# New transfer and matmul estimates in a list planner, and a reserve that now holds for every engine

## The chip, the core and the metric

The kernel runs on one core of a Trainium2 chip. The time is the device time of one execution in microseconds; the median of three runs is given. PE is the matrix engine, DVE, ACT and POOL are the vector, scalar and GpSimd engines, and SP is the engine whose queue issues all transfers here.

## The reference

Two layers are run, each an attention block and a Fourier block, both with a residual and a layer norm in front:

```python
x = A_x                                   # 2048 x 512, 32 heads of 16, 4 segments of 512 rows
for _ in range(2):
    x = x + A(layernorm(x), wq, wk, wv, wo, beta)
    x = x + B(layernorm(x), dft_seq_re, dft_seq_im, dft_hid_re, dft_hid_im)

def A(x, ...):                            # for each segment s, with the memory M, z of those before it
    p = softmax(q_s @ k_s.T * scale + mask);  a_dot = p @ v_s
    a_mem = (phi(q_s) @ M) / (phi(q_s) @ z + 1e-6)
    o_s = g * a_mem + (1 - g) * a_dot
    M, z = M + phi(k_s).T @ v_s, z + sum(phi(k_s))
    # phi(t) = t + 1 where t > 0, else exp(t);   result: concat(o) @ wo

def B(x, ...):                            # real part of a two-dimensional DFT, as matmuls
    a, b = x @ hid_re.T, x @ hid_im.T
    return seq_re @ a - seq_im @ b
```

## The kernel before

**The work.** Eight heads make a group, so a layer has 4 segments x 4 groups and the program 32 groups, numbered i = 0 to 31 (16 to a layer). A group passes through generator functions, each of which yields what it needs next and then issues instructions:

- `s_ln`/`t_ln` normalise four 128-row tiles of a segment and transpose them by a transfer (tile `g`).
- `s_p` multiplies by the q and k weights, `t_split` cuts the product into two fp16 halves, writes them to DRAM (`d<-w`) and reads them back in another layout (`qst<-d`, `kst<-d`). `t_phi` and `t_phk` form phi; `t_phk` starts from a transposed copy of k (tile `kt`, shown as `w<-w`), which POOL adds, ACT and DVE scale, and POOL adds again.
- `s_x` makes scores for the row maxima: PE writes a PSUM tile (kind `ss`, at most 4 held), and `t_max` on DVE takes the maximum with the mask (`junk<-b,cmask`, then `mx`). A transpose of `mx`, two small instructions on `mhl` and four small transfers put the maxima into `qst`. `s_st` then makes the scores again, ACT takes the exponential, POOL cuts the upper triangle (`t_sel`), and `s_av` multiplies by v.
- `s_m` and `t_merge` divide: the denominators go out and come back as [128, 32] (`den<-w` twice, `dc<-den`), DVE takes the reciprocal, `rec<-dc` writes it, `w<-rec` reads it back spread over partitions (tile `z`, kind `mz`), and POOL or DVE multiplies. `s_o` applies `wo`.
- `s_ab`, `s_c`, `s_r`, `s_f` are the Fourier block: `s_c` prepares the sequence matrix, `s_f` multiplies piece by piece into `y` through `t_y`. Of these matmuls there are plenty, and they need little else, so they stand between the others where they can ("the filler", below).

**What sets the order.** No order is written out by hand. A planner runs while the program is built. `Plan.op` keeps for each engine the time at which it is free and for each tile the times of its last write and read, by an estimated cost for each instruction. `Plan.ready` gives the estimated time at which a generator's next step has its inputs and buffers. The loop at the end of `body` always issues the step whose estimated start is earliest. What it issues goes to the end of its engine's queue, and each engine runs its own queue in that order. So a wrong estimate changes no result and no amount of work; it only places an instruction in a queue ahead of one that could have run.

A transfer's estimate in `Plan.op` is issue time `c`, 650 ns, the bytes at 360 bytes per ns on one shared resource `D`, and a `tail`. `est=(c, tail)` sets both at a call. `RESERVE` adds 1000 ns to the readiness of tiles that a transfer wrote and 500 ns to those that POOL wrote, but only where the waiting step is one of PE:

```python
RESERVE = dict(G=500.0, Y=1000.0, V=0.0, A=0.0)
...
            r = max(r, self.wr.get(n, 0.0) + (RESERVE.get(self.by.get(n), 0.0) if eng == "T" else 0.0))
```

All instructions are recorded through one helper (`call` in `Eng`), so the profile puts nearly all of them on line 237; they are told apart by their tiles.

Of the kernel before, what the change touches and what calls it, by code (L numbers as in the profile page):

```python
# [8 lines left out]
F32R = mybir.dt.float32r  # L9
# [30 lines left out]
class Plan:  # L40


    LAT = dict(T=197.0, V=150.0, A=165.0, G=100.0, Y=0.0)

    def __init__(self):
        self.free = dict.fromkeys("VGATYD", 0.0)
        self.acc = {}
        self.cols = {}
        self.wr = {}
        self.rd = {}  # L50
        self.area, self.count, self.slot = {}, {}, {}
        self.fresh = set()
        self.fine = {}
        self.by = {}
        self.dma = None
        self.mode, self.units, self.begun, self.entered = "m", {}, 0.0, 0.0

    def turn(self, mode):
# [65 lines left out]
    def ready(self, reads, tags, eng):  # L124
        r = self.slots_free(tags)
        if r is None:
            return None
        for t in reads:
            n = self.key(t)
            if n in self.fresh:  # L130
                return None
            r = max(r, self.wr.get(n, 0.0) + (RESERVE.get(self.by.get(n), 0.0) if eng == "T" else 0.0))
        return r

    def op(self, eng, name, args, kw):
        aps = [a for a in list(args) + list(kw.values()) if isinstance(a, bass.AP)]
        out, ins = [aps[0]], aps[1:]
        if name == "tensor_tensor_reduce":
            out.append(ins.pop())
        n = max(a.free_size() for a in aps)  # L140
        lat = self.LAT[eng]
        src = any(a.space == bass.MemoryType.PSUM for a in ins)
        if eng == "T":
            n, w = out[0].free_size(), aps[1]
            slow = 4 if w.dtype == F32 else 1
            c = n / 2.4 * slow + (18 if w.dtype == F32R else 3)
            cols = n * slow * w.partition_size() / 128
            mode, unit = "m", 0
            if name == "matmul" and out[0].partition_size() == 32:
                mode, unit = "v", out[0].start_partition() // 32  # L150
            elif w.partition_size() <= 64:
                mode, unit = "h", w.start_partition() // 64
        elif eng == "A":
            c = n / 1.2 + (52 if src else 93) + (93 if any(a.free_size() == 1 for a in ins) else 0)
        elif eng == "V":
            c = 68 + n / 0.96
            if name == "reciprocal":
                c = 68 + n * 6.25
            elif name == "scalar_tensor_tensor" and out[0].dtype == F32:
                c += 60  # L160
            elif name == "tensor_copy" and out[0].dtype == F16:
                c = 68 + n / 1.92
            elif name == "tensor_scalar" and out[0].dtype == F32:
                c = 68 + n / (0.87 if src else 1.32)
        elif eng == "G":
            c = 127 + n * 0.915 if name == "affine_select" else 96 + n * 2.2
            if name == "tensor_tensor" and kw.get("op") == OP.pow:
                c = 300 + n * 165
            elif name == "partition_all_reduce":
                c = 370  # L170
        else:
            stored = out[0].space == bass.MemoryType.DRAM
            c, tail = self.dma or (440, 350 if stored else 950)
            if kw.get("transpose"):
                c, tail = 1350, 450
        t = self.free[eng]
        for a in ins:
            t = max(t, self.wr.get(self.key(a), 0.0))
        for o in out:
            m = self.key(o)  # L180
            t = max(t, self.rd.get(m, 0.0))
            if eng == "V" and "reduce" not in name or self.by.get(m, eng) != eng:
                t = max(t, self.wr.get(m, 0.0))
        psum = [self.key(a) for a in aps if a.space == bass.MemoryType.PSUM]
        for m in psum:
            for o, u in self.acc.get(m, {}).items():
                if o != eng:
                    t = max(t, u)
        if eng == "T":
            if mode == self.mode:  # L190
                t = max(t, self.begun + 7, self.units.get(unit, 0.0))
            else:
                t = max(t, max(self.units.values(), default=0.0) + SWITCH)
                self.mode, self.units, self.entered = mode, {}, t
            k = int(t / TICK)
            if self.cols.get(k - 1, 0) < 3060:
                c = min(2 * c, max(c, (k + 1) * TICK - t + c / 2))
            self.cols[int((t + c) / TICK)] = self.cols.get(int((t + c) / TICK), 0) + cols
        e = t + c
        self.free[eng] = e  # L200
        if eng == "T":
            self.begun = t
            self.units[unit] = e
            if len(self.units) < dict(m=1, h=2, v=4)[mode]:
                self.free[eng] = t + 7
            else:
                self.free[eng] = min(self.units.values())
        if eng == "Y":
            self.free["D"] = max(self.free["D"], e + 650) + out[0].nbytes() / 360
            e = self.free["D"] + tail  # L210
        e += lat
        for m in psum:
            self.acc.setdefault(m, {})[eng] = e
        for a in ins:
            m = self.key(a)
            self.rd[m] = max(e, self.rd.get(m, 0.0))
        for o in out:
            m = self.key(o)
            self.wr[m] = e
            self.by[m] = eng  # L220
            self.fresh.discard(m)
        for a in ins + out:
            if a.tensor.name in self.slot:
                ar, b = self.slot[a.tensor.name]
                ar["last"][b] = max(ar["last"][b], e)
# [18 lines left out]
def body(ctx: ExitStack, tc: tile.TileContext, x, wq, wk, wv, wo, beta, wd, cs, out):  # L244
# [303 lines left out]
    def t_merge(e, o, gi, g, n, key):  # L548
        yield gate("GM")
        yield need("A", e, o, gm, tag=("md", "md"))  # L550
        ds = []
        for src in (e, o):
            d = sb("md")
            A.activation(d, src, AF.Copy)
            ds.append(d)
        A.activation(n, e, AF.Copy, scale=gm[:, gi, 0, g:g + 1])
        yield need("V", n)
        V.scalar_tensor_tensor(n, o, gm[:, gi, 1, g:g + 1], n, op0=OP.mult, op1=OP.add)
        pl.close(e, o)
        yield need("Y", *ds)  # L560
        den = tc.dram_tile([NP, 2, 512], F32)
        rec = tc.dram_tile([NP, 2, 512], F32)
        for a, d in enumerate(ds):
            Y.dma_start(den[:, a, :], d[16 - 16 * a:128:32, :], est=(530, 500))
        pl.close(*ds)
        yield need("Y", den)
        c = rg("dc", 3, F32, (128, 32))
        Y.dma_start(c, den.rearrange("p a (x c) -> (p a x) c", c=32), est=(350, 750))
        yield need("V", c)
        if not gi:  # L570
            V.tensor_scalar(c, c, 1e-6, None, op0=OP.add)
        V.reciprocal(c, c)
        yield need("Y", c)
        Y.dma_start(rec.rearrange("p a (x c) -> (p a x) c", c=32), c, est=(380, 450))
        yield need("Y", rec, tag="mz")
        z = sb("mz")
        Y.dma_start(z, rec.rearrange("p a n -> (p a) n").unsqueeze(1).to_broadcast([2 * NP, 16, 512]),
                    est=(650, 2100))
        yield need("VG", n, z)
        tt(n, n, z, OP.mult)  # L580
        pl.close(z)
        done.add(key)

    def t_split(p, key, f, kphi):
# [16 lines left out]
        yield need("Y", hl)  # L601
        d = tc.dram_tile([2, 2, 64, 512], F16)
        for a in range(2):
            Y.dma_start(d[a].rearrange("j p n -> p j n"), hl[64 * a:64 * a + 64], est=(670, 800))
        pl.close(hl)
        i = key[1]
        if i >= NR:
# [6 lines left out]
        for a in range(2):  # L614
            f = d[a].rearrange("j (d p) n -> (j d) (p n)", p=NP)
            o = dst[64 * a:64 * a + 64].rearrange("r p n -> r (p n)")
            if order:
                Y.dma_start(o[0:32], f, est=(420, 1300))
                Y.dma_start(o[32:48], f[0:16], est=(420, 1300))
            else:  # L620
                Y.dma_start(o[0:16], f[0:16], est=(420, 1300))
                Y.dma_start(o[16:48], f, est=(420, 1300))
        done.add(key)

    def t_phi(p, hl, r, f, key):
# [151 lines left out]
    def s_x():  # L777
        for i in range(NGRP):
# [30 lines left out]
            for a in range(2):  # L809
                for j in range(2):  # L810
                    r = 64 * a + 62 + j
                    Y.dma_start(qs[r:r + 1].rearrange("o p (t n) -> o (p t) n", t=TT),
                                mhl[16 * a:16 * a + 16, j, :], est=(610, 500))
            done.add(("X", i))

    def t_sel(sp, pt, w, n, f, keys):
# [347 lines left out]
```

## Time and profile before

| | us |
|---|---|
| runs | 1836.32, 1828.71, 1827.49 |
| median | 1828.71 |
| span of the profiled execution, first to last instruction | 1824.8 |
| PE busy in the span | 1697.8 (93%) |
| DVE, ACT, POOL busy | 1085.9, 897.1, 724.6 |
| transfers' share of the 16 engines | 47% |

The time of the profiled execution itself isn't listed beside the runs; its span is 3.9 us under their median. PE is the busiest engine by far, and from about 1572 us on it works alone with the filler. PE's own row "PEclk" gives the granted clock, which is under 1 in places early and around 1000 to 1125 us.

### The profile page before, as it was taken

How to read it: one execution, taken by the hardware profiler on the slowest of the kernel's cores; microseconds unless marked ns; L12 is line 12 of the kernel's file. 1: busy time of each engine (PE TensorE's matmuls, PEld its weight loads, DVE VectorE, ACT ScalarE, POOL GpSimd, SP SyncE). 2: the span in 40 equal slices, each digit the busy share in tenths (PEclk: the TensorE clock that was granted, in tenths of full speed). 3: DMA queues.
4: the chain of work that ended last, by engine and by line, in shares of the span. 5: the costliest groups of instructions: out<-in, count | busy, mean ns of one | idle time of the engine just before them, and what ended most of it. 6: DMA issues, size and time to landing. Idle time of an engine off the chain costs nothing. (4 is left out here: it accounts for less than half of the span.)

```text
span 1824.8 us, 32643 instructions
## 1 busy us (share of the span) xinstructions
PE 1697.8 (93%) x11045; PEld 742.2 (41%) x11045; DVE 1085.9 (60%) x3404; ACT 897.1 (49%) x1563; POOL 724.6 (40%) x1158
## 2 busy tenths in 40 slices
PE   3878799989989999999999879999999999999999
PEld 2433334443433434344444333434444434444444
DVE  7786955577765877565556655564656567533211
ACT  2557656757465666644436655555445444431000
POOL 3234545546363464553434543442534334231000
PEclk8988899999999999999999898999999999999999
DMA  7345535655454653345784541553544444222233
GB/s 190 105 135 132 170 74 165 156 152 150 127 147 136 191 149 102 119 151 167 232 226 156 136 124 49 144 131 100 132 110 114 141 120 102 83 84 81 93 122 115
DMA packets 240985, 242.44 MB, mean 133 GB/s; under 512 B 129777, under 2 KB 152305, under 8 KB 240817
## 3 DMA queue, kind: packets, MB, share of 16 engines
q1 hardware_dynamic: 240816, 240.35, 46.9%
q8 instruction: 87, 1.43, 0.3%
q14 instruction: 82, 0.66, 0.1%
HBM read 152.96 MB, written 63.70 MB: 119 GB/s over the span
## 5 line engine op out<-in xcount | busy, mean ns | idle before, releaser
L237 PEld LDWEIGHTS <-w 128*128 128x128 f16 x4992 | 463.8, 98 | 613.3 <-issue 113.0
L237 PE MATMUL b<-w,w 128*128 128x512 f16 x3072 | 708.9, 380 | 2.0 <-ACT w L237 1.7
L237 POOL TENSOR_TENSOR w<-w,w 128x512 f16<-128x512 f32 (+1 forms) x316 | 380.6, 1208 | 412.6 <-ACT w L237 266.9
L237 ACT ACTIVATE w<-b,fac 128x512 f32<-128x512 f32 (+1 forms) x728 | 420.9, 658 | 176.6 <-PE b L237 156.0
L237 DVE CUSTOM_DVE_ANT_0 junk<-b,cmask 128x128 bf16<-128x128 f32 (+3 forms) x1024 | 437.6, 485 | 77.7 <-PE b L237 76.3
L237 POOL TENSOR_SCALAR_AFFINE_SELECT w<-w 128x128 f32<-128x128 f32 (+2 forms) x704 | 242.4, 357 | 309.5 <-ACT w L237 302.6
L237 DVE SCALAR_TENSOR_TENSOR y<-b,fyu,y 128x512 f32<-128x512 f32 x200 | 149.2, 746 | 217.7 <-PE b L237 217.2
L237 ACT ACTIVATE w<-b 128x512 f32<-128x512 f32 (+1 forms) x240 | 138.2, 600 | 251.9 <-PE b L237 240.4
L237 ACT ACTIVATE w<-w,csc 128x512 f16<-128x512 f32 (+1 forms) x256 | 181.1, 721 | 60.7 <-DVE csc L237 51.5
L237 PE MATMUL b<-g,w 128*128 128x512 f16 x768 | 190.4, 391 | 7.4 <-DMA g<-w 5.8
L237 PE MATMUL b<-w,vt 128*32 128x512 f32 (+3 forms) x2048 | 186.2, 460 | 3.0 <-POOL w L237 2.2
L237 PE MATMUL b<-wd,w 128*128 128x512 f16 x768 | 178.7, 380 | 0.9 <-DVE w L237 0.5
L237 ACT ACTIVATE w<-w 128x512 f16<-128x512 f32 (+1 forms) x144 | 90.7, 635 | 168.5 <-DVE w L237 117.4
L237 DVE SCALAR_TENSOR_TENSOR w<-b,w 128x512 f16<-128x512 f32 x128 | 88.1, 688 | 132.6 <-ACT w L237 131.9
L237 PE MATMUL b<-kst,qst 62*128 62x128 f16 (+3 forms) x1024 | 131.9, 314 | 25.3 <-DMA kst<-d 10.0
L237 PE MATMUL b<-qst,kst 64*128 64x512 f16 (+3 forms) x1024 | 123.8, 308 | 16.4 <-ACT w L237 6.1
L237 PE MATMUL b<-w,g 128*128 128x128 f16 x1536 | 99.5, 224 | 10.9 <-DVE mx L237 4.8
L237 PEld LDWEIGHTS <-g 128*128 128x128 f16 x1536 | 91.2, 100 | 25.1 <-issue 14.5
L237 PEld LDWEIGHTS b<-w,vt 128*32 128x32 f32 x2048 | 55.9, 111 | 101.0 <-issue 56.4
L237 PEld LDWEIGHTS <-kst 64*128 64x128 f16 x1024 | 38.3, 95 | 137.2 <-issue 124.7
L237 PE MATMUL b<-wo,w 128*128 128x512 f16 x384 | 89.7, 379 | 0.2 <-ACT w L237 0.2
L237 DVE DVE_READ_ACCUMULATOR2_ANT mx<- 128x1 f32 x1024 | 84.5, 83 | 0.0
(102 smaller groups left out, 887.1 us busy)
## 6 DMA issues: line engine op xcount, KB each, us to landing
w<-in_cs_dram SPq DMA_DIRECT2D x128, 256.0 KB
cc<-w SPq DMA_DIRECT2D x128, 256.0 KB
w<-cc SPq DMA_DIRECT2D x128, 256.0 KB
w<-w SPq DMA_DIRECT2D x96, 256.0 KB
d<-w SPq DMA_DIRECT2D x128, 128.0 KB
w<-rec SPq DMA_DIRECT2D x56, 256.0 KB
w<-in_x_dram SPq DMA_DIRECT2D x32, 256.0 KB
qst<-d SPq DMA_DIRECT2D x64, 128.0 KB
```

The source lines that it names most:

```text
L237: r = f(*args, **kw)
```

## The change

New numbers go into the planner's table, and one condition falls. No instruction of the computation is added or taken away.

- The reserve of 1000 ns behind transfers and 500 ns behind POOL now holds for steps of all engines, SP included.
- A transfer's estimate has three parts: issue `c`, then 590 ns, then `took` on the shared resource `D`, then `tail`. `took` is set for each kind. SP's next transfer is not estimated to start before the eighth transfer back has landed.
- `LAT`, the delay from an instruction's end to its consumer, changes for all engines.
- The matmuls on 32-column strips (`s_av`) are estimated as two at a time at half the cost, where they were four at a time; fp32 matmuls on 64 rows likewise one at a time at half the cost. POOL's cost per element goes from 2.2 to 2.1 ns.

```diff
-    LAT = dict(T=197.0, V=150.0, A=165.0, G=100.0, Y=0.0)
+    LAT = dict(T=235.0, V=115.0, A=150.0, G=85.0, Y=25.0)
...
-            r = max(r, self.wr.get(n, 0.0) + (RESERVE.get(self.by.get(n), 0.0) if eng == "T" else 0.0))
+            r = max(r, self.wr.get(n, 0.0) + RESERVE.get(self.by.get(n), 0.0))
...
-            c = n / 2.4 * slow + (18 if w.dtype == F32R else 3)
+            c = max(n / 2.4 * slow, 200 if slow > 1 else 0) + (18 if w.dtype == F32R else 3)
...
-                mode, unit = "v", out[0].start_partition() // 32
+                mode, unit, c = "v", out[0].start_partition() // 32 % 2, c / 2
             elif w.partition_size() <= 64:
                 mode, unit = "h", w.start_partition() // 64
+                if slow > 1:
+                    unit, c = 0, c / 2
...
-            c, tail = self.dma or (440, 350 if stored else 950)
+            c, took, tail = self.dma or ((415, 917, 364) if stored else (470, 829, 755))
+            took *= out[0].nbytes() / 262144 if self.dma is None else 1
             if kw.get("transpose"):
-                c, tail = 1350, 450
+                c, took, tail = 1325, 850, 300
...
+        if eng == "Y" and len(self.lands) >= 8:
+            t = max(t, self.lands[-8])
...
         if eng == "Y":
-            self.free["D"] = max(self.free["D"], e + 650) + out[0].nbytes() / 360
+            self.free["D"] = max(self.free["D"], e + 590) + took
             e = self.free["D"] + tail
+            self.lands.append(e)
...
-        Y.dma_start(c, den.rearrange("p a (x c) -> (p a x) c", c=32), est=(350, 750))
+        Y.dma_start(c, den.rearrange("p a (x c) -> (p a x) c", c=32), est=(413, 0, 776))
...
-                    est=(650, 2100))
+                    est=(709, 1909, 899))
```

The same instructions then stand in other places. Three places are shown; buffer numbers differ between the two programs, names stand for the same things.

SP at the start of the program, where the four normalised tiles (`w4` to `w6`, `w8`) are transposed into `g0` and the first split weights are stored (`w00`, `w10`). Before:

```order
L237 DMA_TRANSPOSE g0_276<-w4_305 128x8x128
L237 DMA_TRANSPOSE g0_276<-w5_308 128x8x128
L237 DMA_TRANSPOSE g0_276<-w6_316 128x8x128
L237 DMA_TRANSPOSE g0_276<-w8_345 128x8x128
L237 DMA w00_128<-w7_344 128x1024
L237 DMA w10_129<-w9_354 128x1024
```

And in the changed program:

```order
L244 DMA_TRANSPOSE g0_276<-w4_307 128x8x128
L244 DMA_TRANSPOSE g0_276<-w5_314 128x8x128
L244 DMA_TRANSPOSE g0_276<-w6_320 128x8x128
L244 DMA w00_128<-w7_346 128x1024
L244 DMA_TRANSPOSE g0_276<-w8_347 128x8x128
L244 DMA w10_129<-w9_355 128x1024
```

The store of the first weights has moved ahead of the fourth transpose.

ACT a little later, from the weights of the first groups (reads of `y`) to the first exponentials of group 0 (reads of `b` with `fac`); `mhl` belongs to the maxima of group 0, and reads of `b` alone are the halves of a product of `s_p`. Before:

```order
L237 ACTIVATE w18_580<-y_84,scl_118 128x512
L237 ACTIVATE vt0_106<-b4_483 128x16x2x16
L237 ACTIVATE w19_681<-y_84,scl_118 128x512
L237 ACTIVATE mhl_677<-b0_675 32x128
L237 ACTIVATE w20_691<-y_84,scl_118 128x512
L237 ACTIVATE w21_712<-b4_683 128x512
L237 ACTIVATE w23_738<-y_84,scl_118 128x512
L237 ACTIVATE w24_747<-b3_743,fac_127 128x512
```

And in the changed program:

```order
L244 ACTIVATE w22_614<-b7_561 128x512
L244 ACTIVATE w23_668<-b5_607 128x512
L244 ACTIVATE vt1_107<-b1_655 128x16x2x16
L244 ACTIVATE w25_748<-y_84,scl_118 128x512
L244 ACTIVATE w26_772<-w21_608,fac_127 128x512
L244 ACTIVATE w21_608<-w21_608 128x512
L244 ACTIVATE w27_821<-y_84,scl_118 128x512
L244 ACTIVATE mhl_817<-b6_815 32x128
L244 ACTIVATE w28_831<-y_84,scl_118 128x512
L244 ACTIVATE w30_888<-b4_823 128x512
L244 ACTIVATE w31_929<-b3_879 128x512
L244 ACTIVATE w32_935<-b5_931,fac_127 128x512
```

The products of group 1 (`w22`, `w23`, `vt1`) and its phi (`w26`, `w21`) have moved ahead of the maxima of group 0, and those of group 2 (`w30`, `w31`) ahead of group 0's exponentials. On PE the matmuls of `s_p` and `s_v` for group 1 accordingly stand between the scores of group 0, ahead of its transpose of `mx`, where they stood behind it.

SP around the division of group 27, deep in the second layer. Before (the first three rows are its denominators on their way out and back):

```order
L237 DMA den_18798<-w43_18738 4x512
L237 DMA den_18798<-w46_18740 4x512
L237 DMA dc_18842<-den_18798 128x32
L237 DMA rec_18799<-dc_18842 128x32
L237 DMA w9_18903<-rec_18799 128x1x512
L237 DMA w37_18910<-cc50_192 128x1024
```

And in the changed program, from the read of `den_18810`, which was written 13 rows further up:

```order
L244 DMA dc_18985<-den_18810 128x32
L244 DMA dc_18989<-den_18908 128x32
L244 DMA w47_19002<-w13_138 128x1024
L244 DMA d_19025<-w38_19009 64x2x512 x2
L244 DMA w22_19040<-cc54_196 128x1024
L244 DMA rec_18909<-dc_18989 128x32
L244 DMA w48_19079<-rec_18909 128x1x512
L244 DMA d_19094<-w43_19075 64x2x512 x2
L244 DMA rec_18811<-dc_18985 128x32
```

Where one step of the division followed directly on the one that it waits for, other groups' transfers stand between. On DVE the reciprocal of this division stood between maxima of 384 columns, with those of 512 columns behind it; now it stands behind the last of the maxima of 512 columns. Over the whole program SP's row `dc<-den` stands directly behind its own `den<-w` in 29 of 56 divisions before and in 15 of 56 now, and `w<-rec` directly behind `rec<-dc` in 19 and 9.

More of the change, by code (lines that the diff above doesn't have):

```diff
@@ L55, in __init__ @@
         self.dma = None
+        self.lands = []
         self.mode, self.units, self.begun, self.entered = "m", {}, 0.0, 0.0
@@ L165, in op @@
         elif eng == "G":
-            c = 127 + n * 0.915 if name == "affine_select" else 96 + n * 2.2
+            c = 127 + n * 0.915 if name == "affine_select" else 96 + n * 2.1
             if name == "tensor_tensor" and kw.get("op") == OP.pow:
@@ L203, in op @@
             self.units[unit] = e
-            if len(self.units) < dict(m=1, h=2, v=4)[mode]:
+            if len(self.units) < dict(m=1, h=2, v=2)[mode]:
                 self.free[eng] = t + 7
@@ L563, in t_merge @@
         for a, d in enumerate(ds):
-            Y.dma_start(den[:, a, :], d[16 - 16 * a:128:32, :], est=(530, 500))
+            Y.dma_start(den[:, a, :], d[16 - 16 * a:128:32, :], est=(596, 204, 313))
         pl.close(*ds)
@@ L573, in t_merge @@
         yield need("Y", c)
-        Y.dma_start(rec.rearrange("p a (x c) -> (p a x) c", c=32), c, est=(380, 450))
+        Y.dma_start(rec.rearrange("p a (x c) -> (p a x) c", c=32), c, est=(417, 530, -74))
         yield need("Y", rec, tag="mz")
@@ L603, in t_split @@
         for a in range(2):
-            Y.dma_start(d[a].rearrange("j p n -> p j n"), hl[64 * a:64 * a + 64], est=(670, 800))
+            Y.dma_start(d[a].rearrange("j p n -> p j n"), hl[64 * a:64 * a + 64], est=(651, 702, 467))
         pl.close(hl)
@@ L617, in t_split @@
             if order:
-                Y.dma_start(o[0:32], f, est=(420, 1300))
-                Y.dma_start(o[32:48], f[0:16], est=(420, 1300))
-            else:
-                Y.dma_start(o[0:16], f[0:16], est=(420, 1300))
-                Y.dma_start(o[16:48], f, est=(420, 1300))
+                Y.dma_start(o[0:32], f, est=(415, 520, 800))
+                Y.dma_start(o[32:48], f[0:16], est=(415, 520, 800))
+            else:
+                Y.dma_start(o[0:16], f[0:16], est=(415, 520, 800))
+                Y.dma_start(o[16:48], f, est=(415, 520, 800))
         done.add(key)
@@ L812, in s_x @@
                     Y.dma_start(qs[r:r + 1].rearrange("o p (t n) -> o (p t) n", t=TT),
-                                mhl[16 * a:16 * a + 16, j, :], est=(610, 500))
+                                mhl[16 * a:16 * a + 16, j, :], est=(609, 341, 172))
             done.add(("X", i))
```

## The prediction

> **What bounds the kernel now.** I began with the page: the span, the busy rows and the chain that ended last.
>
> ```profile
> span 1824.8 us, 32643 instructions
> PE 1697.8 (93%) x11045; PEld 742.2 (41%) x11045; DVE 1085.9 (60%) x3404; ACT 897.1 (49%) x1563; POOL 724.6 (40%) x1158
> PE 27%; DMA 2%; DVE 2%; issue 1%; POOL 1%; ACT 1%; SPq 0%; DVEq 0%; ACTq 0%; POOLq 0%
> ```
>
> PE does the same 11045 matmuls in either order, so the change can only act on what PE loses: 127 us of idleness, and time at a lower clock. Next I cut the span where the work changes, by the windows.
>
> ```profile
> 0.00:52.00 52.00, 21.73 (x121) 11.26 (x121) 40.58 (x148) 10.12 (x17) 15.15 (x22) 0.90 0.63 167
> 52.00:237.00 185.00, 152.19 (x1087) 64.84 (x1087) 142.47 (x502) 114.08 (x204) 75.17 (x143) 0.86 0.48 136
> 237.00:1000.00 763.00, 734.73 (x4768) 327.47 (x4767) 491.30 (x1462) 446.49 (x753) 369.77 (x520) 0.99 0.54 154
> 1000.00:1125.00 125.00, 105.10 (x796) 41.98 (x795) 77.60 (x294) 71.37 (x130) 53.91 (x112) 0.88 0.44 115
> 1125.00:1572.00 447.00, 435.08 (x3023) 186.99 (x3020) 262.35 (x884) 217.12 (x393) 179.04 (x311) 1.00 0.45 117
> 1572.00:1824.80 252.80, 248.98 (x1259) 109.69 (x1255) 71.59 (x119) 37.96 (x68) 31.52 (x52) 1.00 0.29 96
> ```
>
> Columns: length, busy PE, weight loads, DVE, ACT, POOL, then the clock. PE is idle 30.3 us up to 52, 32.8 up to 237 and 19.9 in 1000 to 1125; these are the bare stretches, with attention and no filler, and there the clock falls to 0.86 to 0.90. With filler at hand PE is idle only 28.3 + 11.9 = 40.2 us in 1210 us. The last 253 us are full and can give nothing. Third view, the waits: whom PE waits for in the two stretches with filler (237 to 1000, then 1125 to 1572; total, times, longest).
>
> ```profile
> PE b L237 <- DVE mx L237: 7.6, 6, 4.8
> PE b L237 <- DVE cam L237: 7.1, 8, 2.2
> PE b L237 <- ACT w L237: 3.9, 8, 0.8
> PE b L237 <- DVE w L237: 2.1, 3, 1.6
> ...
> PE b L237 <- DVE mx L237: 4.5, 7, 1.4
> PE b L237 <- ACT w L237: 2.9, 5, 1.2
> PE b L237 <- DVE w L237: 1.7, 2, 1.3
> ```
>
> These rows sum to 29.8 us behind DVE and ACT, which are themselves idle for a third of that time and more. Fourth view, the timeline at three such waits, to see why an engine with time to spare is late: around 379, 1251 and 1467 us (the bracket is the idle time just before, and what ended it).
>
> ```profile
> 381.32 1.15 POOL L237 TENSOR_TENSOR w<-w 128x512 f32<-128x512 f16 x1 [2.90 <-DMA w<-w]
> 382.51 0.72 ACT L237 ACTIVATE w<-w,fac 128x512 f32<-128x512 f32 x1 [4.49 <-POOL w L237]
> 383.26 0.49 DVE L237 TENSOR_SCALAR w<-w,fac 128x512 f32<-128x512 f32 x1 [4.32 <-ACT w L237]
> 383.66 0.55 DVE L237 CUSTOM_DVE_ANT_0 junk<-b,cmask 128x384 bf16<-128x384 f32 x1
> 384.26 1.99 PE L237 MATMUL b<-w,g 128*128 128x128 f16 x17 [4.79 <-DVE mx L237]
> ...
> 1248.87 1.26 POOL L237 TENSOR_TENSOR w<-w,w 128x512 f32<-128x512 f32 x1 [6.40 <-DMA w<-rec]
> 1251.66 0.63 ACT L237 ACTIVATE w<-w 128x512 f16<-128x512 f32 x1 [3.40 <-POOL w L237]
> 1252.81 0.27 PE L237 MATMUL b<-kst,qst 62*128 62x256 f16 x1 [1.18 <-ACT w L237]
> ...
> 1467.52 0.36 DVE L237 RECIPROCAL dc<-dc 128x32 f32<-128x32 f32 x1 [3.94 <-DMA dc<-den]
> 1467.79 0.49 DVE L237 CUSTOM_DVE_ANT_0 junk<-b,cmask 128x384 bf16<-128x384 f32 x1
> 1468.35 0.85 PE L237 MATMUL b<-kst,qst 62*128 62x512 f16 x2 [1.23 <-DVE mx L237]
> ```
>
> At all three, an instruction that needs a transfer, or POOL behind a transfer, stands at the head of a queue. Maxima or exponentials stand behind it, and PE waits for those.
>
> **The reserve (gain).** Of a division's links, the chain view shows these (start, length).
>
> ```profile
> 1244.87 3.86 DMA w<-rec
> 1461.22 3.03 DMA den<-w
> 1464.31 3.19 DMA dc<-den
> ```
>
> The planner reckoned `dc<-den` at 350 + 650 + 45 + 750 = 1.80 us and put the reciprocal there; it took 3.19, and DVE stood 3.94 us. The new estimate is hardly longer (413 + 590 + 776 + 25 = 1.80), but the reserve adds 1.00, so the reciprocal is placed 2.80 us behind, and 0.39 us of the error stays. On `w<-rec` old and new sums are 4.13, near the 3.86 measured, so there the reserve is slack. In the phi of k it adds 1.00 at POOL, 0.50 at ACT and 0.50 at DVE, up to 2.0 of the 4.3 us that DVE stood at 379. What it moves back is not free: behind each of these links wait the rest of the division and `s_o`, which come later. With filler at hand that costs nothing, since `s_f` covers it.
>
> How much of the 29.8 us goes? Nothing at the one end (new waits of the same size arise in the new order), all at the other. Nearest are the three places shown, 4.79 + 1.18 + 1.23 = 7.2 us; the links at them recur in every group, though most of their errors never reach PE. I take 10 us, a third. Direct waits of PE for transfers had the reserve already and count nothing.
>
> The price of the `dc<-den` link can also be had from a rule. The Trainium skill (DMA: Bandwidth & Descriptors, section "Anatomy of one DMA — SWDGE (gpsimd) path") fits a transfer at about 2.0 us fixed plus bytes over 436 GB/s, hence an estimate of 2.04 us for 16 KB. By that the 2.80 us would leave no error and this term would be about 10.4 us; by the row 0.39 us of 1.23 stays at such a place. The row, from SP's queue and not POOL's, decides.
>
> **The clock behind those waits (gain).** The clock falls after longer waits of PE; here behind the one at 379 and one at 582.
>
> ```profile
> 384.00:391.00 7.00, 6.74 (x56) 5.57 (x57) 3.98 (x13) 1.01 (x2) 1.26 (x1) 0.57 0.60 186
> 585.00:591.00 6.00, 5.64 (x33) 1.88 (x34) 4.27 (x27) 0.00 (x0) 0.00 (x0) 0.50 0.26 63
> ```
>
> Each lost about 3 us (7 x 0.43, 6 x 0.50). The first is behind a wait that I take as gone: 3.0 us. The second followed a wait for `kst<-d` itself and stays. Ends: 0 and 6.
>
> **The start (gain and loss).** Up to 56 us DVE sets the pace: it is full while PE runs out of work.
>
> ```profile
> 41.00:56.00 15.00, 8.83 (x69) 4.72 (x69) 14.77 (x75) 1.81 (x3) 0.00 (x0) 0.84 0.01 5
> 55.80 0.39 PE L237 MATMUL b<-identf,mx 128*32 128x128 f32 x1 [3.91 <-DVE mx L237]
> ```
>
> The new order puts the products of group 1 between the scores of group 0, ahead of the transpose that waited 3.91 us. That work fills the wait: 3.9 us, if DVE isn't late again later (then 0; at most the 6.2 us that PE idles in these 15). Against it, the fourth transpose is behind the store of the first weights on SP.
>
> ```profile
> 9.35 7.59 SPq L237 DMA_TRANSPOSE g<-w  x4
> 17.04 1.39 SPq L237 DMA_DIRECT2D w<-w  x2
> 18.87 8.23 PE L237 MATMUL b<-g,w 128*128 128x512 f16 x24 [5.79 <-DMA g<-w]
> ```
>
> PE's first products wait for these transposes, so the store's 0.7 us (half of 1.39) and a wait for its own input come in front: I take 0.8 us lost, between 0.7 and 1.5.
>
> **The layer boundary (nothing).** In 1000 to 1125 us PE waits for DVE's maxima and for `kst<-d`.
>
> ```profile
> PE b L237 <- DVE mx L237: 10.9, 9, 6.5
> PE b L237 <- DMA kst<-d: 4.1, 2, 3.9
> ```
>
> The new order puts more of group 21's products and group 19's value products ahead of the first scores of group 20, and fills the 3.9. But its maxima on DVE then start about as late, and the transpose waits for them as before. What is gained at the first wait is lost at the second: I take 0, between -4 and +4.
>
> **Edits with no term.** The strip matmuls' two units at half cost give the planner the same total, and the new costs of POOL and the `LAT` values move starts by 15 to 40 ns; they only break ties. The eight-transfer limit spreads SP's rows. With filler these changes are covered by `s_f`; in the bare stretches that cover is missing, which is the slower rival below.
>
> **The sum.** -10 - 3.0 - 3.9 + 0.8 + 0 = -16.1 us on the span of 1824.8, or 1808.7. The median stands 3.9 us over the span, so 1812.6: 1813 us, 0.9% faster.
>
> **Rivals.** About 0.5% (9.1 us) is what a measurement of this kernel can tell from no change: under 1819.6 is faster, over 1837.9 slower.
>
> *No difference.* DVE bounds the bare stretches by its amount of work (77% busy in 52 to 237, full in 41 to 56), and with filler a new order has its own late links, since an error of 0.39 us stays on `dc<-den` and the estimates of the rest are no longer or shorter than before. For it: the largest lost blocks are bare ones. Against it: the reserve demonstrably separates links in SP's order. It gives 1829.5 (start +0.8, the rest cancelled), between 1820 and 1838. It is also the case in which the change doesn't do what it says, because a step that has no competitor is issued at the same place, reserve or not.
>
> *Slower.* Place: 52 to 237. In the new order ACT's first exponentials, and with them POOL's cuts and the value products of group 0, come behind the products of group 2. On PE some 28 us of work stand ahead of them, where 17 stood (matmuls counted in the order, at 216 ns for 512 columns, the pace of the full rows here).
>
> ```profile
> 1700.00:1825.00 125.00, 121.11 (x562) 54.70 (x559) 23.20 (x32) 2.39 (x4) 0.00 (x0) 0.99 0.30 105
> ```
>
> If ACT and POOL can't catch up, the segment's end, `s_o` and the first filler come 11 us later, 12.8 at a clock of 0.86: 1828.7 + 12.8 = 1841.5. It decides if ACT becomes full: it would have to do its 114 us in the 185 less some 11 and stay in step. At 62% busy that is against it; for it speaks that the clock falls further when PE waits.
>
> *Much faster.* All 40.2 us with filler go, and both clock losses: 1828.7 - 40.2 - 6 - 3.1 = 1779. Against it: the direct waits for transfers had their reserve before.
>
> **How the numbers follow.** Forecast 0.49, with 1795 to 1822 its own range; no difference 0.27; slower 0.18; much faster 0.06. Faster: 0.47 of the forecast, 0.06 of the last and 0.02 of the second make 0.55. Slower: 0.17 of its rival and 0.03 of the second, 0.20. The rest, 0.25, is within 0.5%. Leaving out a tenth at each side gives 1787 (between forecast and much faster) to 1843 (just past the slower rival).
>
> **What would show it.** In the trace after: DVE's wait for `dc<-den` halved from its 54.4 us, and POOL's for `w<-rec` well under 104.9.
>
> ```profile
> POOL w L237 <- DMA w<-rec: 104.9, 37, 19.9
> DVE dc L237 <- DMA dc<-den: 54.4, 26, 5.2
> ```
>
> PE's idle time with filler should fall from 40 to about 30 us, the first products start near 19.7 us and not 18.9, and the transpose of group 0's maxima wait under 1 us. The boundary should lose about as much as before. The prediction is wrong if the idle time with filler stays, or if the bare stretch before the first filler grows.

## The result, and the profile after

The changed kernel takes 1799.18 us (median of four runs, 1797.41 to 1799.37), the kernel before 1828.1 beside it (1825.83 to 1836.32): ratio 0.983, 95% interval 0.9808 to 0.9851. 1813 us was forecast, 15.7 under the median of before that was known then (1828.71); it gained 28.9. The sign is right and the time lies in the range, but the size is off, and the runs below show that the reason given for it is wrong too.

The page of the changed kernel, the three rows that answer to the first fence of the prediction:

```profile
span 1797.4 us, 32675 instructions
PE 1696.4 (94%) x11045; PEld 741.8 (41%) x11045; DVE 1084.2 (60%) x3409; ACT 899.0 (50%) x1563; POOL 719.3 (40%) x1153
PE 43%; DVE 2%; issue 1%; ACT 1%; DMA 1%; SPq 1%; POOL 1%; DVEq 0%; ACTq 0%; POOLq 0%
```

PE does the same 11045 matmuls in 1696.4 us of busy time, 1.4 less than before; 26 of the 27.4 us of span come out of its idleness, 127 before and 101 now. By stage, in the windows of before (start and end, length, busy PE, weight loads, DVE, ACT, POOL, then clock, transfers' share, GB/s):

```profile
0.00:52.00 52.00, 24.58 (x165) 14.46 (x166) 41.31 (x137) 12.11 (x20) 14.87 (x22) 0.93 0.68 186
52.00:237.00 185.00, 145.55 (x1078) 62.11 (x1076) 140.42 (x510) 113.88 (x204) 77.19 (x146) 0.85 0.51 133
237.00:1000.00 763.00, 751.63 (x4918) 332.91 (x4916) 497.75 (x1510) 459.01 (x775) 374.40 (x538) 0.99 0.55 157
1000.00:1125.00 125.00, 110.03 (x706) 43.14 (x704) 74.26 (x264) 66.47 (x122) 50.58 (x101) 0.82 0.39 97
1125.00:1572.00 447.00, 442.93 (x3086) 191.09 (x3088) 267.54 (x890) 217.41 (x390) 175.80 (x307) 1.00 0.46 121
1572.00:1797.40 225.40, 221.70 (x1107) 98.04 (x1099) 62.88 (x102) 30.15 (x54) 26.43 (x41) 1.00 0.30 98
```

With filler PE is idle 11.4 + 4.1 = 15.4 us, 40.2 before. The bare stretch from 52 to 237 is worse, 39.4 us idle after 32.8, and the clock at the layer boundary fell from 0.88 to 0.82. Since equal windows don't hold equal work, I also cut both traces where PE has done the same work (matmuls in the order of the trace, weighted by their columns at full clock). Where the pieces are divided matters by a few us, most of all between the start and the bare stretch, where the two kernels are ahead of each other by turns; so the sizes are rough. They put the difference here: the start -6.5 us, the bare stretch +8.6, the first layer with filler -22.3 (785.0 to 762.7), the boundary +3.1, the rest -10.8 (698.5 to 687.7). The gain lies where there is filler, and start and bare stretch together come to about nothing.

The waits that the prediction named, after:

```profile
POOL w L244 <- DMA w<-rec: 47.0, 16, 13.5
DVE dc L244 <- DMA dc<-den: 9.7, 11, 3.3
```

Both fell further than foretold (104.9 and 54.4 before). By this view alone the prediction's first term looks confirmed. It is not, as the first two experiments show.

### The profile page after: what moved, and what is told of

It reads as the page before. It is cut to its first block, busy times and chain, and to the rows that moved or that the text cites. A ratio compares the mean times of both kernels' runs of the same rounds, so it can differ in the third digit from the quotient of the medians.

```text
span 1797.4 us, 32675 instructions
## 1 busy us (share of the span) xinstructions
PE 1696.4 (94%) x11045; PEld 741.8 (41%) x11045; DVE 1084.2 (60%) x3409; ACT 899.0 (50%) x1563; POOL 719.3 (40%) x1153
## 4 chain that ended last, share of the span: by engine, by line
PE 43%; DVE 2%; issue 1%; ACT 1%; DMA 1%; SPq 1%; POOL 1%; DVEq 0%; ACTq 0%; POOLq 0%
PE b L244 43%; ACT w L244 1%; DVE junk L244 1%; SPq L244 1%; DMA w<-w 1%; POOL w L244 1%; DVE w L244 0%; DMA w<-rec 0%; DVE mx L244 0%; DVE y L244 0%; DMA dc<-den 0%; DMA w<-in_cs_dram 0%; DVE dc L244 0%; DVE bst L244 0%; POOL rs L244 0%
## 5 line engine op out<-in xcount | busy, mean ns | idle before, releaser
L244 POOL TENSOR_TENSOR w<-w,w 128x512 f16<-128x512 f32 (+1 forms) x312 | 375.8, 1211 | 343.6 <-ACT w L244 255.3
L244 PE MATMUL b<-w,vt 128*32 128x512 f32 (+3 forms) x2048 | 190.6, 471 | 2.7 <-POOL w L244 1.3
L244 PEld LDWEIGHTS b<-w,vt 128*32 128x32 f32 x2048 | 58.0, 113 | 98.3 <-issue 56.6
L244 PEld LDWEIGHTS <-kst 64*128 64x128 f16 x1024 | 38.7, 96 | 142.8 <-issue 124.5
```

The source lines that it names most:

```text
L244: r = f(*args, **kw)
```

## The experiments

R stands for the theory of the prediction, that the reserve makes the gain; E for the new estimates (E1 transfers, E2 value products), J for chance of the order. Each kernel runs the same instructions of the computation in another order. "Idle" is PE's idle time in the windows 237 to 1000 and 1125 to 1572 together, and the last two columns are the waits of DVE for `dc<-den` and of POOL for `w<-rec`, all from the profiled execution of the run; the ratio is to the kernel before on the same chip. Different runs used different chips, on which the median of before went from 1822.5 to 1828.1 us, so that ratios compare better than medians.

| run | median us | ratio (95%) | idle | dc | rec |
|---|---|---|---|---|---|
| before | 1828.1 | | 40.2 | 54.4 | 104.9 |
| after | 1799.2 | 0.983 (0.9808-0.9851) | 15.4 | 9.7 | 47.0 |
| e1 reserve only | 1820.8 | 0.9991 (0.9969-1.0012) | 31.1 | 35.8 | 47.2 |
| e2 estimates only | 1809.2 | 0.9925 (0.9896-0.9953) | 18.1 | 34.7 | 89.2 |
| e3 before, 5 ns | 1824.8 | 1.0004 (0.9984-1.0023) | 32.1 | 40.1 | 77.1 |
| e4 after, 5 ns | 1829.3 | 1.0027 (1.001-1.0043) | 30.9 | 14.6 | 38.7 |
| e5 transfers only | 1801.4 | 0.9887 (0.9857-0.9917) | 20.1 | 45.9 | 99.4 |
| e6 products only | 1823.3 | 0.999 (0.9972-1.0009) | 33.7 | 58.7 | 119.9 |
| e7 after, 5 ns elsewhere | 1824.6 | 0.9997 (0.9978-1.0016) | 26.8 | 13.4 | 45.3 |
| e8 estimates, 5 ns | 1807.1 | 0.9918 (0.9894-0.9943) | 17.1 | 32.4 | 67.1 |
| e9 limit of eight only | 1825.9 | 1.0027 (1.0006-1.0047) | 32.9 | 55.2 | 89.9 |
| e10 transfers, no limit | 1806.5 | 0.9918 (0.99-0.9936) | 19.1 | 37.0 | 74.9 |
| e11 transfers, old share | 1823.2 | 0.9999 (0.9982-1.0016) | 26.3 | 45.6 | 102.7 |
| e12 transfers + reserve | 1807.4 | 0.9919 (0.9897-0.9942) | 19.8 | 19.0 | 56.8 |
| e13 share only | 1807.0 | 0.9898 (0.986-0.9937) | 17.0 | 25.8 | 98.3 |
| e14 share of `w<-rec` | 1815.6 | 0.9952 (0.9931-0.9972) | 25.9 | 49.8 | 91.3 |
| e15 share of plain transfers | 1824.0 | 0.9995 (0.9973-1.0017) | 27.8 | 45.1 | 82.2 |
| e16 after, 5 ns, third place | 1804.2 | 0.9885 (0.985-0.992) | 15.9 | 14.1 | 32.0 |
| e17 share of `w<-rec` and halves | 1802.9 | 0.9898 (0.9873-0.9923) | 18.4 | 36.2 | 87.4 |
| e18 e4 with `cam` 3 us later | 1824.1 | 1.0009 (0.9991-1.0026) | 24.7 | 8.6 | 48.5 |

### Is it the reserve? (e1, e2)

e1 puts the new reserve alone into the kernel before; e2 is the changed kernel with the old one.

```diff
 e1, on before (e2: the reverse, on after)
-            r = max(r, self.wr.get(n, 0.0) + (RESERVE.get(self.by.get(n), 0.0) if eng == "T" else 0.0))
+            r = max(r, self.wr.get(n, 0.0) + RESERVE.get(self.by.get(n), 0.0))
```

> The kernel before with one line changed: the reserve holds for every engine; all old estimates stay. Theory R (the reserve takes blocked heads out of the queues, and my term for it was too small): about 1803 us (1796 to 1810), PE's idle time in 237 to 1000 us falls from 28.3 to under 16 us, DVE's wait for dc<-den from 54.4 to under 20. Theory E (the new estimates do it): 1820 to 1830, idle time in that window above 22 us. Theory J (any reshuffle of this order moves the time by 1%): no prediction from the edit, 1810 to 1845.

> The changed kernel with the reserve back on PE's steps alone; all new estimates stay. Theory R: 1820 to 1830 us, PE's idle time in 237 to 1000 above 22 us, DVE's wait for dc<-den above 40. Theory E: 1797 to 1806, idle time there under 16. Theory J: anywhere from 1790 to 1845.

The reserve alone halves POOL's wait and takes a third off DVE's, in the waits of e1:

```profile
POOL w L237 <- DMA w<-rec: 47.2, 23, 5.5
DVE dc L237 <- DMA dc<-den: 35.8, 22, 4.3
```

The time doesn't follow: ratio 0.9991. In the windows of e1 PE still idles 31 us with filler, 19.9 of them in the first stretch, where R had expected under 16 and E above 22:

```profile
237.00:1000.00 763.00, 743.07 (x4809) 326.25 (x4807) 490.70 (x1482) 446.10 (x755) 367.93 (x528) 0.99 0.53 154
1125.00:1572.00 447.00, 435.86 (x3028) 187.11 (x3028) 260.56 (x876) 216.62 (x388) 174.83 (x305) 0.99 0.46 119
```

R falls. That the idle time with filler is 9 us less than in before says little, since kernels as slow as before show 25 to 40 us of it in the table. The estimates alone give 0.9925 while POOL still waits 89.2 us (1809.2 us, 3 above what E had expected): it is the estimates that gain, and not through these waits.

### How far does chance of the order go? (e3, e4, e7, e8, e16)

```diff
 e3, on before
-    LAT = dict(T=197.0, V=150.0, A=165.0, G=100.0, Y=0.0)
+    LAT = dict(T=197.0, V=150.0, A=170.0, G=100.0, Y=0.0)
 e4 on after, e8 on e2: A=155.0 for 150.0;  e7 on after: T=240.0 for 235.0;  e16 on after: G=90.0 for 85.0
```

> The kernel before with a single planner number moved by 5 ns (the delay behind ACT, 165 to 170), which reorders about a quarter of the rows and has no reason to help or harm. Theories R and E: within 8 us of 1828 (1820 to 1836), PE's idle time in 237 to 1000 within 8 us of 28.3. Theory J: 10 to 25 us away from 1828 on either side.

> The changed kernel with the same 5 ns step (150 to 155). Theories R and E: within 8 us of 1799 (1791 to 1807), PE's idle time in 237 to 1000 within 6 us of 11.4. Theory J: 10 to 25 us above 1799, back among the times of the kernel before.

> The changed kernel with another single planner number moved by 5 ns (the delay behind PE, 235 to 240). If the changed kernel's 1799 was what its edits bring and the first such step an unlucky one: 1795 to 1810. If it was a lucky order out of a spread (theory J): 1812 to 1835, with PE's idle time and half clock up in the bare stretch 52 to 237 or somewhere in 237 to 1000, another place than in the first jitter.

> The estimates without the wider reserve, with the delay behind ACT moved by 5 ns (150 to 155). Theory E (the estimates are worth some 15 us whatever the order): 1800 to 1818 us, idle in 1125 to 1572 under 6. Theory J: 1790 to 1840, and its distance to 1809 of the size of the edits' own.

> The changed kernel with one delay moved by 5 ns in another place (LAT of POOL 85 to 90). The shipped order took 1799, two neighbours 1829 and 1825, and the transfers with the reserve 1807. If the shipped time is the rule and the two neighbours the exception: 1795 to 1805. If the reserve makes the order of the bare stretch a matter of chance: anything from 1795 to 1832; a slow one should again show PE waiting about 5 us for DVE's cam between 170 and 215 us and a clock near 0.6 behind it.

On before and on e2 5 ns change little (1.0004; 0.9918 beside 0.9925). On the changed kernel they cost 30, 25 and 5 us by the medians, the first more than the 10 to 25 expected of J. e4 parts the waits from the time most clearly: its waits are nearly as short as after's, and it is as slow as before.

```profile
POOL w L244 <- DMA w<-rec: 38.7, 13, 13.7
DVE dc L244 <- DMA dc<-den: 14.6, 12, 4.2
```

Where e4 loses: cut at equal work, the bare stretch differs by 3.7 us only (15.2 lost in the piece at about 109 to 230 us, 11.0 given back in the next), but the first layer with filler takes 788.3 us where after has 762.7. One place of it, in the windows and the timeline of e4:

```profile
520.00:560.00 40.00, 33.92 (x206) 15.64 (x207) 33.60 (x106) 15.69 (x27) 17.67 (x18) 0.87 0.40 108
```

```profile
546.28 0.69 DVE L244 CUSTOM_DVE_ANT_0 junk<-b,cmask 128x512 bf16<-128x512 f32 x1
546.89 0.08 DVE L244 DVE_READ_ACCUMULATOR2_ANT mx<- 128x1 f32 x1
546.89 1.27 DVE L244 TENSOR_REDUCE cam<-w 128x1 f32<-128x512 f32 x2
547.03 0.39 PE L244 MATMUL b<-identf,mx 128*32 128x128 f32 x1 [3.70 <-DVE mx L244]
```

DVE has been working without a break for 13 us, mostly on maxima, with `cam` (the maxima of the filler's sequence matrix) and pieces of `y` between, and PE stands 3.70 us for the last of the maxima. No transfer and no POOL stands in that stretch of DVE's work, so a shorter wait for a transfer doesn't help here. The slow neighbours e4 and e7 also share a mark in the bare stretch, where PE waits about 5 us for `cam` (5.05 and 5.24). In e4, with 18 score matmuls behind:

```profile
188.59 0.56 PE L244 MATMUL b<-cam,ones 128*128 128x4 f32 x2 [5.05 <-DVE cam L244]
189.09 1.78 PE L244 MATMUL b<-kst,qst 62*128 62x128 f16 x18
```

The granted clock of e4 behind it is 0.59 for 20 us; the changed kernel has 1.00 in this window and waits 1.22 us for such a product, but 0.67 in the 20 us after that, where e4 has 0.88.

```profile
190.00:210.00 20.00, 15.45 (x64) 4.09 (x61) 19.12 (x77) 15.70 (x28) 13.88 (x24) 0.59 0.58 179
```

e18, below, was to ask whether that mark is a cause.

### Which estimate? (e5, e6, then e9 to e11)

```diff
 e5, on before: all hunks on transfers (590, took, tail, every est=, the limit of eight), nothing else
 e6, on before: the strip matmuls as two units at half cost, fp32 on 64 rows, the floor of 200; nothing else
```

> The kernel before with the new transfer estimates alone (issue, 590 ns, took, tail, the limit of eight); reserve for PE alone, old value products, old delays. Theory E1 (of the estimates it is the transfers): 1806 to 1814 us, like the estimates all together (1809), and PE's idle time in 1125 to 1572 under 6 us (11.9 before). Theory E2 (the value products): 1820 to 1830, idle there above 9. Theory J (chance of the order, 15 us either way): no prediction beyond 1800 to 1840.

> The kernel before with the new cost of the fp32 matmuls alone (two strips at a time at half the cost, 64-row fp32 likewise). Theory E1: 1820 to 1830 us, PE's idle time in 1125 to 1572 above 9 us. Theory E2: 1806 to 1814, idle there under 6. Theory J: 1800 to 1840.

E2 falls (0.999), E1 holds (0.9887, all that e2 has; with 1801.4 us it is 5 us under the range expected). In e5 the waits are nearly those of before, and yet PE's idleness with filler is halved, by its windows:

```profile
POOL w L242 <- DMA w<-rec: 99.4, 27, 12.9
DVE dc L242 <- DMA dc<-den: 45.9, 29, 6.3
```

```profile
237.00:1000.00 763.00, 747.46 (x4823) 330.08 (x4821) 496.84 (x1490) 449.18 (x760) 370.58 (x525) 1.00 0.55 156
...
1125.00:1572.00 447.00, 442.43 (x3110) 189.07 (x3107) 269.56 (x897) 221.19 (x399) 173.63 (x312) 1.00 0.44 115
```

The transfer estimates have three parts: the limit of eight, the time of a transfer by itself, and the share (`took`) for which it holds the planner's one resource `D`, so that the next transfer is planned to land later.

```diff
 e9, on before (`lands` lists when the transfers land)
+        if eng == "Y" and len(self.lands) >= 8:
+            t = max(t, self.lands[-8])
 e10: e5 without these two lines
 e11: e5 with the old share; a transfer alone lands at the same time as in e5
-            self.free["D"] = max(self.free["D"], e + 590) + took
-            e = self.free["D"] + tail
+            old = out[0].nbytes() / 360
+            self.free["D"] = max(self.free["D"], e + 590) + old
+            e = self.free["D"] + tail + took - old
```

> The kernel before, and of the change only this: SP's next transfer is not estimated to start before the eighth transfer back has landed. All transfer estimates are the old ones. Theory L (the limit is what the new transfer estimates gain, since it spreads SP's rows): about 1802 us, like the kernel with all transfer estimates (1801.4). Theory S (the gain is the longer occupation of the shared resource, took, so that transfers that follow each other closely are planned to land later): within 0.5% of before, 1820 to 1834. Theory T (the gain is the corrected time of a transfer by itself, issue plus tail): also 1820 to 1834.

> The kernel before with all new transfer estimates but without the limit of eight. Theory L: back near before, 1820 to 1834. Theories S and T: the gain stays, 1795 to 1810.

> The kernel before with the new transfer estimates and the limit of eight, but each transfer holds the shared resource only as long as before (its bytes at 360 per ns); what took is longer or shorter than that goes into its tail, so a transfer by itself is planned to land at the same time as with the new estimates. Theory S: back near before, 1818 to 1832. Theories L and T: the gain stays, 1795 to 1810. Theory J (chance of the order; each new order falls somewhere within 15 us or so whatever the numbers mean): no relation to the pieces, any of the three runs may come out fast or slow.

The limit alone gives nothing (1.0027), without it the gain stays (0.9918), and with the old share it is gone (0.9999). Theory S, the share, is the one left.

### The share alone, and whose (e13, e14, e15, e17)

```diff
 on before; {...} holds old est -> new took, as named; a transfer alone lands as before
-            self.free["D"] = max(self.free["D"], e + 650) + out[0].nbytes() / 360
-            e = self.free["D"] + tail
+            old = out[0].nbytes() / 360
+            took = {...}.get(self.dma, old)
+            self.free["D"] = max(self.free["D"], e + 650) + took
+            e = self.free["D"] + tail + old - took
 e13: all kinds;  e14: {(650, 2100): 1909};  e15: plain transfers, 917 and 829 per 256 KB
 e17: {(650, 2100): 1909, (670, 800): 702, (420, 1300): 520}
```

> The kernel before; of the change only the share that each transfer takes of the planner's one transfer resource (took in place of bytes at 360 per ns). The time of a transfer by itself stays as before, since the tail is shortened by what the share grew; no limit of eight. Theory S (this share is the whole gain): 1797 to 1810. If S needs the corrected times as well: between 1810 and 1820. Theory J (chance): about 1823.

> As the run before, but with the longer share for the read of the reciprocals (w<-rec) alone, 1909 ns in place of 728. If that read, whose share was furthest off, carries the gain: 1797 to 1810. If it is the plain transfers of 256 KB: 1818 to 1830.

> As the run before, but with the longer share for the plain transfers alone (917 ns for a store of 256 KB and 829 for a load, in place of 728). If the plain transfers carry the gain, since there are most of them and the filler's matrix comes by them: 1797 to 1810. If it is the reads of the reciprocals, or the halves (d<-w, qst<-d, kst<-d): 1818 to 1830. If it needs several: both this run and the one before between 1808 and 1820.

> The kernel before with the longer share for the read of the reciprocals (w<-rec) and for the split halves on their way out and back (d<-w, qst<-d, kst<-d); the plain transfers keep the old share. The reciprocals alone gave 1815.6 us, the plain transfers alone nothing, all together 1807.0. If the halves carry the missing part: 1802 to 1811. If they add nothing, and the rest needs the plain ones after all: 1812 to 1820.

The share alone gives 0.9898, as much as all transfer estimates. The read of the reciprocals by itself is worth half (0.9952, between the two ranges expected), with the split halves it is the whole (0.9898), and the plain transfers by themselves give nothing (0.9995). The halves alone were not run. The windows of e17:

```profile
237.00:1000.00 763.00, 747.92 (x4875) 330.47 (x4875) 509.29 (x1529) 455.14 (x771) 372.87 (x541) 1.00 0.53 154
...
1125.00:1572.00 447.00, 443.64 (x3111) 190.79 (x3110) 271.03 (x900) 223.65 (x402) 176.18 (x311) 1.00 0.44 119
```

That the read of the reciprocals holds the transfer engines longer could be read from the trace of before. Its windows at the read issued at 1244.87, and at the six plain reads `w<-cc` queued behind it (the last two columns are the transfers' share and GB/s):

```profile
1246.20:1247.80 1.60, 1.60 (x9) 0.76 (x8) 0.00 (x0) 1.60 (x5) 0.00 (x0) 1.00 0.55 186
1247.80:1250.60 2.80, 2.80 (x16) 1.01 (x14) 0.00 (x0) 0.45 (x1) 1.73 (x3) 1.00 1.02 350
```

At 186 GB/s its 262144 bytes take 1.41 us; at the 350 that the plain reads move together, the same bytes take 0.75. The planner before reckoned 0.73 for both, the new one 1.91 and 0.83. While the read runs only 0.55 of the engines' time is busy. The Trainium skill (DMA: Bandwidth & Descriptors, section "Why a DMA increments its semaphore by 16 and not by 1") says that a transfer is spread over the largest number of engines, up to 16, that divides the slowest dimension (of a size over 1) of both sides; the source of `w<-rec` has 8 rows outermost, which by that gives 8 of 16. The 0.55 agrees with it; no run here tried another layout.

### Reserve and estimates together (e12, e18)

```diff
 e12: e5 with the reserve for every engine
 e18: e4, and in s_c ahead of the product of the maxima
+            if not k:
+                pl.wr[pl.key(cam)] += 3000.0
             yield need("T", cam, tag="dft")
```

> The new transfer estimates with the limit, and the reserve for every engine; no new value-product estimates and no new delays. If the reserve adds to the transfer estimates by its own mechanism: 1795 or less. If what the changed kernel has over the estimates alone is the luck of one order, as its two neighbours (1829.3 and 1824.6 us) suggest: 1800 to 1830, no better than the transfer estimates alone (1801.4).

> The changed kernel with ACT's delay moved by 5 ns (1829.3 us), and the planner told that the first maxima of the filler's matrix (cam) come 3 us later, so that their product no longer stands on PE 5.05 us ahead of them. If this one place, with the clock of 0.59 behind it, is what the neighbour lost in the stretch up to 237 us: PE doesn't wait over 2 us for cam there, and 1808 to 1818 (5 us of waiting and some 8 of the slower clock gone, the rest of its loss stays further on). If the loss only moves to another wait: 1822 to 1832.

e12 has both and is no better than e5 (1807.4 beside 1801.4). In e18 PE still stands 3.98 us ahead of such a product, a wait that is now put down to the maxima `mx`, and the clock stayed low; its timeline and its windows:

```profile
189.88 0.59 PE L244 MATMUL b<-cam,ones 128*128 128x4 f32 x2 [3.98 <-DVE mx L244]
```

```profile
190.00:210.00 20.00, 17.82 (x56) 4.72 (x57) 15.12 (x65) 12.06 (x22) 11.76 (x22) 0.62 0.36 106
```

With 1824.1 us the expectation of 1808 to 1818 is missed. But e18 took neither the wait nor the low clock away, so it can't tell by itself what the place is worth. Two other things speak against it as the cause. e4 gave back in the next piece most of what it lost there, which I had not set against it. And e16, which is fast with 1804.2 us, has nearly the same mark at 213 us, with a clock of 0.57 behind it; its timeline and its windows:

```profile
213.44 0.59 PE L244 MATMUL b<-cam,ones 128*128 128x4 f32 x2 [4.51 <-DVE cam L244]
```

```profile
210.00:230.00 20.00, 13.93 (x63) 4.17 (x64) 15.63 (x67) 9.64 (x17) 7.76 (x16) 0.57 0.20 59
```

e15 shows the wait (5.00 us) without the reserve, so the mark doesn't belong to the reserve either.

## Why the prediction was right or wrong

- **The reserve, -10 us: wrong.** The working took the waits of DVE and POOL for transfers to be the cause of PE's waits with filler. They shrank as foretold, but e1 has them at 35.8 and 47.2 with ratio 0.9991, e4 at 14.6 and 38.7 with 1.0027, and e5 has them long with 0.9887. The three places shown summed to 7.2 us of PE's time; nothing shows that such waits, taken away, leave PE busy, and e4 shows PE behind a DVE that waits for no transfer. By itself the term measured -1.6 us, not to be told from 0 (-5.7 to +2.2 us by the interval).
- **Transfer estimates, nothing: wrong, and the step that failed.** "The new estimate is hardly longer" (of `dc<-den`) and "On `w<-rec` old and new sums are 4.13" compared the time of a transfer alone, which hardly changes. That `took` also takes the place of bytes/360 on the shared resource, 1909 ns for 728 at `w<-rec`, was in the diff and is named under "The change", and I gave it no term. It measures 18.6 us of gain (e13: 0.0102 of 1825.2, interval 11.5 to 25.6). "The estimates of the rest are no longer or shorter than before" in the first rival is the same error.
- **Limit of eight, strip matmuls: nearly right** (e9 1.0027, a loss of 1 to 9 us; e6 0.999). `LAT` and POOL's cost as ties: wrong on this kernel, where 5 ns in `LAT` moved the changed kernel by 5 to 30 us, right on before and on e2. The new `LAT` values and POOL's new cost were not run alone; e2, which has them beside the transfers, is no better than e5.
- **Clock behind the waits, -3.0: not separable.** From 237 to 900 us the granted clock went from 0.99 to 1.00 here, but along with the idle time of the same stretch (24.2 to 8.4 us), and up to 1000 us it is 0.99 in both.
- **The start, -3.9 and +0.8: right in kind, too small.** Cut at equal work the start gains about 6.5 us. The first products come at 20.49, not at the foretold 19.7, behind a wait of 7.04 us where it was 5.79, so the loss was 1.6 and not 0.8. But the transpose of the first maxima waits 0.22 us in place of 3.91, and from 41 to 56 us PE is busy 13.18 us where it was 8.83. Timeline and windows of after:

```profile
20.49 7.85 PE L244 MATMUL b<-g,w 128*128 128x512 f16 x24 [7.04 <-DMA g<-w]
...
62.30 0.40 PE L244 MATMUL b<-identf,mx 128*32 128x128 f32 x1 [0.22 <-DVE mx L244]
```

```profile
41.00:56.00 15.00, 13.18 (x113) 7.71 (x114) 13.89 (x66) 4.65 (x8) 1.07 (x1) 1.00 0.46 125
```

- **The slower rival: its place was right, its reason not.** The bare stretch did grow, which the prediction had named as a sign of being wrong: by 8.6 us of the 12.8 reckoned in the pieces above, but by only 1 to 3 us if they are divided at 52 and 237 us of before. ACT is no fuller there (113.88 us after 114.08). What grew is PE's wait for the small transfers that bring the maxima, of which the rival says nothing, while its wait for the maxima themselves fell from 13.2 to 4.1 us. PE's waits from 52 to 237 us (total, times, longest), before and then after:

```profile
PE b L237 <- ACT w L237: 6.3, 14, 1.3
...
PE b L237 <- DMA qst<-mhl: 0.9, 1, 0.9
```

```profile
PE b L244 <- DMA qst<-mhl: 9.3, 5, 5.6
...
PE b L244 <- ACT w L244: 4.5, 7, 1.5
```

- **The boundary, 0: right within its bounds** (+3.1, between -4 and +4), but not for the reason given. PE's wait for `mx` fell as well, from 10.9 to 6.5 us, and that for `kst<-d` is gone; against it stands the lower clock, 0.82 after 0.88.

So the gain of 1.7% is made up of about 1.0% by the share of the reads of the reciprocals and of the split halves, which six orders with at least these shares and the old reserve have (e2, e5, e8, e10, e13, e17: 1801 to 1809) and none without them (e1, e3, e6, e9, e11, e15: 1821 to 1826), and 0.7%, the difference, that is this order's own: luck, as far as the runs show. Of the six orders with shares and the reserve, three took 1799 to 1807 (after, e12, e16) and three 1824 to 1829 (e4, e7, e18), so with the reserve the gain of the shares was lost as often as it was kept. What of the order decides between the two groups stays open: the one wait that the slow ones had in common is in e16 too. By which waits the longer share helps is not shown either, only that PE's idleness with filler goes with it: 15 to 20 us in all faster kernels from 1799 to 1809, 25 to 40 in all others. Among those others it doesn't set the time: e18 with 24.7 us and e11 with 26.3 are no faster than before with 40.2.

## What to carry to other kernels

In a list planner the time for which a transfer blocks the next can matter more than its own latency; compare both with the trace, for each kind, by the rate in the windows where it runs alone. A wait that shrinks on an engine with time to spare is no gain until the busy engine's idle time over the whole span shrinks too. Where one order is measured, move an unimportant number by a few ns and measure the neighbours, since one good order says little about the rule that made it.

## What was not expected of the hardware

The read of the reciprocals runs at 186 GB/s with the engines 0.55 busy, where plain reads reach 350 at 1.02. A wait of PE of 5.05 us in the bare stretch of e4 was followed by 20 us at a granted clock of 0.59, though no single wait in them was over 1.3 us. And 5 ns in a planner's table made 30 us by the medians, without one instruction more or less in the computation.
